# Thirteen small constants and the choice of the fixed expert, spread over pairs of heads, and four steps of the tail and the slots put elsewhere

## The chip, the core and the metric

The kernel runs on one core of a Trainium2 chip. The metric is the time of one execution on the device, in microseconds (us). Before the change it was 640.17 us, the median of three runs (639.43 to 644.14). The core's engines work from queues of their own, each in program order, and meet at semaphores: PE is TensorE (matrix products), DVE is VectorE, ACT is ScalarE, POOL is GpSimd, and SP issues most DMA transfers.

## The reference

```python
def reference(**kwargs):
    ...
    attn_out = _attn_ref(**attn_kwargs)          # 4 batches, 8 heads, 576 tokens, head size 64
    B, H, S, D = attn_out.shape
    x = attn_out.transpose(0, 2, 1, 3).reshape(B * S, H * D)      # 2304 tokens x 512
    x = _moe_ref(x=x, **moe_kwargs)
    return _moe2_ref(x=x, **moe2_kwargs)

def _attn_ref(q, k, v):                          # heads 0-3: the last 32 tokens,
    scores = scale * np.matmul(q, k.transpose(0, 1, 3, 2))        # heads 4-7: each 4th of the last 128
    scores = np.where(masks[None], scores, -1000000000.0)
    attn = np.exp(scores - scores.max(-1, keepdims=True))
    attn = attn / (np.sum(attn, axis=-1, keepdims=True) + 1e-09)
    return np.matmul(attn, v)

def _moe_ref(x, w_gate, w_output_gate, w1, w2):  # 8 experts, F = 1024, one expert for each token
    logits = x @ w_gate
    e_idx = np.argmax(logits, axis=1)
    ...
    for e in range(E):
        h = np.maximum(x[mask] @ w1[e], 0.0)
        out[mask] = gate_w[mask, None] * eom[mask, e, None] * (h @ w2[e])
```

The second MoE (`_moe2_ref`) is like the first, with a bias by modality added to the logits and without the output gate `eom`.

## The kernel before

**Attention** goes over 16 pairs of heads. `iteration(n)` is software pipelined: it holds the steps of several neighbouring pairs, in the order of a list of names written out by hand (`ORDER`). Of pair n+1 it computes scores (`stA`, 'A0' to 'A2', into `ps`), of which DVE takes row maxima `M` (line 399); POOL splits the maxima into three bf16 parts (`r`, `mb`, lines 415 to 420, step 'MS'), and PE turns them (`pm`, line 430, step 'MT') so that they can be subtracted in the transposed scores of pair n (`stB`). Of pair n-1 it computes the value product (`stC`, 'C0' and 'C1', into `po`, line 459), and DVE normalises it: `rc` (463), `recip` (465), `xh` (466). After that come the low half of `x` on POOL (481), transposes, and the router's logits (`stR`, 530 and 531). The splits of the keys (`kk`, 356) and queries (`qs`, `ql`) of pair n+2 lie between these on DVE and POOL. The order on DVE in an iteration is: two `M`, `rc`, `recip`, `xh`, `kk`, `M`, `qs`, `kk`, `ql`.

Two places in `iteration(n)` take further work: its start, ahead of the first two `M`, and the entry 'W' of `ORDER`, between `xh` and the first `kk`. At the start of iteration 3 stood `slot_consts()` and `token_values()`, 13 small operations that turn the iota tile in `cft` into tables of slot numbers (`slots`, `tokv`; 153 to 170), which only the sort needs. From iteration 8 on `fes`, the generator of `first_expert("a")`, is advanced at both places. It counts, over the first 512 tokens, which expert is chosen most: seven DVE operations on `fe_eqa` (186 to 192), a matmul `pfe` (195), four on `fe_mea` (198 to 201), five on POOL that end in the expert's number `fe_gia` (205 to 210), and three on DVE (`fe_Mia`, `fe_Msa`, `fe_owna`). At the 'DW' of iteration 10 SP reads that number and starts to load this expert's weights.

**The tail** is the last pairs' steps, written out in `tail()`, with the raw weights' splits (`los`, `his`, line 107) and `first_slots` (`fs()`, names `fs_`) among them. The latter finds 256 tokens of the fixed expert in the first 1664: it ends in a comparison `fs_A` (230), a matmul `pfs` (275), the indices `fs_fidx` (278) and two gathers on POOL.

**Each MoE** works in slots of 128 tokens of one expert. Slots 0 and 1 belong to the fixed expert; meanwhile `sort()` places all other tokens (generators `so1`, `so2`), with a matmul `pidx` (834) and `idx` (838), gathers of the first sorted slots, and the table of experts by slot that the weights are loaded by. A slot is: gathered rows turned by PE (`pxt`, 918) and copied by ACT (`xT`, 919), first product `ph` (940), ReLU and its remainder (`hh`, `hl`), second product `py` (1012), and output `y`. In the first MoE, the output is also turned (`pyt`, 1174) and sent through the second router (`plg`, 1183, added on DVE by `lg`, 1192). Weights are split into f16 halves on ACT (102) and DVE (107). `at(s, k, ...)` puts a call at place k of slot s. The first 18 slots always run (`NMIN`); the others lie in nested branches on the number of slots, each with a branch hint ahead of it. In this input the first MoE takes 23 slots and the second 19.

Of the kernel before, what the change touches and what calls it, by code (L numbers as in the profile page):

```python
# [11 lines left out]
F32 = mybir.dt.float32  # L12
# [27 lines left out]
HINT = [mybir.EngineType.PE, mybir.EngineType.DVE]  # L40
# [15 lines left out]
def fused(ctx, tc, qk, vw, wr1, w1a, w2a, mid, wr2, mbias, w1b, w2b, cf, c16, cbs, cms, cib, out, dbg=None):  # L56
# [93 lines left out]
    def slot_consts():  # L150
        v = nc.vector
        si, so = (lg2.rearrange("p s e -> p (s e)")[:, k * NSLOT:(k + 1) * NSLOT].bitcast(I32) for k in range(2))
        v.tensor_copy(si, iota_t)
        v.tensor_scalar(so, si, 1, None, op0=ALU.bitwise_and)
        v.tensor_scalar(si, si, 1, None, op0=ALU.logical_shift_right)
        v.tensor_copy(s_odd, so)
        v.tensor_copy(s_half, si)
        v.tensor_scalar(s_even, s_odd, -1.0, 1.0, op0=ALU.mult, op1=ALU.add)
        v.tensor_tensor(s_even, s_even, s_half, op=ALU.mult)
        v.tensor_scalar(s_even, s_even, -1.0, None, op0=ALU.add)  # L160
        v.tensor_scalar(s_half, s_half, KA - 1.0, None, op0=ALU.add)
        v.tensor_scalar(s_two, iota_t, 2.0, None, op0=ALU.mult)
        v.memset(s_half[:, 0:1], 0.0)
        v.memset(s_odd[:, 1:2], 0.0)
# [11 lines left out]
    def first_expert(nm, lg0, psum, fe):  # L176
# [5 lines left out]
        def T(name, shape, dt=F32):  # L182
            return const.tile(shape, dt, name=f"fe_{name}{nm}")
        sh = [P, n, E]
        mx, eq, mi, me, cnt = T("mx", [P, n]), T("eq", sh), T("mi", [P, n]), T("me", [P, E]), T("cnt", [P, E], F16)
        v.tensor_reduce(out=mx, in_=lg0, axis=AX.X, op=ALU.max)
        v.tensor_tensor(eq, lg0, mx.unsqueeze(2).to_broadcast(sh), op=ALU.is_equal)
        v.tensor_tensor(eq, eq, desc.unsqueeze(1).to_broadcast(sh), op=ALU.mult)
        v.tensor_reduce(out=mi, in_=eq, axis=AX.X, op=ALU.max)
        v.tensor_tensor(eq, eq, mi.unsqueeze(2).to_broadcast(sh), op=ALU.is_equal)  # L190
        v.tensor_reduce(out=me, in_=eq.rearrange("p t e -> p e t"), axis=AX.X, op=ALU.add)
        v.tensor_copy(cnt, me)
        yield
        pm = psum()
# [7 lines left out]
        yield  # L202
# [92 lines left out]
    with ExitStack() as actx:  # L295
# [152 lines left out]
        def stC(n, h):  # L448
# [11 lines left out]
            if h == 0:  # L460
                return
            rc = ap2.tile([QT, 2, NQ, 1], F32, name="rc")
# [100 lines left out]
        def tail():  # L563
# [25 lines left out]
            stX(a, 0)  # L589
            stX(a, 1)  # L590
            fs()
            stC(b, 1)
            fs()
            stH(b)
            fs()
# [11 lines left out]
        def iteration(n):  # L607
# [14 lines left out]
            if n == 3:  # L622
                nc.gpsimd.tensor_copy(midf, midt[:, :, 0])
                slot_consts()
                token_values()
            if n >= fe_:
                next(fes, None)
            for o in ORDER:
                if o == 'W':
                    if n >= fe_:  # L630
                        next(fes, None)
# [33 lines left out]
        actx.enter_context(tc.manual_schedule())  # L665
        for n in range(-4, NPR - 1):
            iteration(n)
# [45 lines left out]
    def sort(nm, lg, nt, inv, fe, ea, tab, scale, og, extra, gscale, start):  # L713
# [127 lines left out]
        for i in range(KA, KA + 3):  # L841
            start.gather(i)
        table()
# [48 lines left out]
    def moe(w1, w2, tab, src, parts, post, start, wpair):  # L892
# [70 lines left out]
        def slot(s, nsl=None):  # L963
# [14 lines left out]
            if NMIN - 1 <= s < NSLOT - 1:  # L978
                tc.mark_branch_hint_location(f"{start.name}{s + 1}", hint=nsl > s + 1, engines=HINT)
# [23 lines left out]
            if s >= KE:  # L1003
                post.turn(s - 1)
            hook(5)
# [5 lines left out]
            for a, w in ops:  # L1011
                nc.tensor.matmul(to, a, w, start=k == 0, stop=k == len(ops) - 1)  # L1012
                k += 1
                if k == 4:
                    hook(9)
                    if s == NMIN - 1:
                        post.router(s - 2)
# [120 lines left out]
    class Post1:  # L1138
# [38 lines left out]
        def router(self, s):  # L1177
            pl = pp.tile([P, E], F32, name="plg", tag="plg")
# [40 lines left out]
    at(0, 10, run(so1, 2))  # L1219
# [8 lines left out]
    at(2, 5, lambda: start1.first_splits(FIRST[3]))  # L1228
# [3 lines left out]
    at(2, 6, first_out(post1, start1, 1))  # L1232
# [31 lines left out]
    class Post2:  # L1264
# [27 lines left out]
        def router(self, s):  # L1292
            pass
# [9 lines left out]
    at(1, 9, run(so2, 2))  # L1303
    at(1, 7, lambda: start2.turned(KA))
# [91 lines left out]
```

## Time and profile before

| | |
|---|---|
| runs | 644.14, 639.43, 640.17 us; median 640.17 |
| profiled execution: its own time | 638.38 us |
| span of its trace | 636.6 us |
| mean granted clock of TensorE | 0.971 |
| attention and tail, to the first MoE's first product | 0 to 150.56 us |
| first MoE, to the second's first product | 150.56 to 419.86 us |
| second MoE | from 419.86 us |

One execution is profiled, and the times in the trace are counted from the span's start. The span is 1.8 us shorter than that execution's own time, and the median of the runs is 1.8 us longer than that again. A granted clock of 1.00 is the full clock of TensorE.

### The profile page before, as it was taken

The page shows a single profiled execution, that of the slowest core. Times are in us where ns is not written, and L with a number is a line of the kernel's source. Part 1 is how long each engine was busy: PE and PEld are TensorE (multiplying, and loading weights), DVE is VectorE, ACT ScalarE, POOL GpSimd, SP SyncE. Part 2 cuts the span into 40 slices and gives each one's busy share as a digit, 9 for nine tenths or more (in the row PEclk, how much of TensorE's full clock was granted, in tenths as well). Part 3 has the DMA queues.
Part 4 walks back from the last instruction along what each step waited for, and adds up shares of the span by engine and source line. Part 5 has one row for each costly group of instructions (what it writes and reads, how often), then busy time and mean ns, then how long its engine had stood idle before and what let it go on. Part 6 is the DMA issues. An engine that isn't in the chain of part 4 may idle for free. (4 is left out here: it accounts for less than half of the span.)

```text
span 636.6 us, 19375 instructions
## 1 busy us (share of the span) xinstructions
PE 589.1 (93%) x7380; PEld 456.1 (72%) x7380; DVE 359.9 (57%) x657; ACT 272.8 (43%) x370; POOL 196.1 (31%) x307
## 2 busy tenths in 40 slices
PE   3888889977999999999999999989999999999994
PEld 2868778867668677687776777856777777777772
DVE  6798898888889327944859732247530101013560
ACT  5677767773294126823538411110632111114550
POOL 2567767613151310111110610002654221212120
PEclk9799989975999999999999999999999999999998
DMA  8766668972499856996968683301994423233921
GB/s 290 243 191 194 211 198 273 293 167 72 146 357 368 226 117 180 378 243 151 266 198 221 169 153 65 69 21 36 324 323 121 99 60 93 63 91 114 300 56 37
DMA packets 100864, 114.15 MB, mean 179 GB/s; under 512 B 64399, under 2 KB 69263, under 8 KB 100752
## 3 DMA queue, kind: packets, MB, share of 16 engines
q1 hardware_dynamic: 95072, 94.89, 52.5%
q0 software_dynamic: 5280, 17.13, 9.1%
q8 instruction: 59, 0.97, 0.6%
q10 hardware_dynamic: 400, 0.72, 0.3%
q14 instruction: 53, 0.43, 0.2%
HBM read 209.13 MB, written 18.22 MB: 357 GB/s over the span
## 5 line engine op out<-in xcount | busy, mean ns | idle before, releaser
L940 PEld LDWEIGHTS <-wb 128*128 128x128 f16 x4032 | 229.7, 98 | 7.3 <-issue 1.5
L940 PE MATMUL ph<-xT,wb 128*128 128x128 f16 x3648 | 210.5, 219 | 1.1 <-ACT xT L919 1.1
L951 DVE SCALAR_TENSOR_TENSOR hl<-ph,hh 128x512 f16<-128x512 f32 x84 | 57.7, 689 | 162.8 <-ACTq L959 152.8
L1012 PE MATMUL py<-wb,hh 128*128 128x512 f16 x608 | 137.8, 379 | 0.0
L950 ACT ACTIVATE hh<-ph 128x512 f16<-128x512 f32 x84 | 50.2, 597 | 147.7 <-PE ph L940 147.3
L1012 PEld LDWEIGHTS <-hh 128*128 128x128 f16 x672 | 63.6, 98 | 68.0 <-ACT hh L950 0.3
L107 DVE SCALAR_TENSOR_TENSOR wb<-raw,wb 128x1024 f16<-128x1024 f32 (+1 forms) x80 | 104.7, 1346 | 12.7 <-ACT wb L102 11.3
L102 ACT ACTIVATE wb<-raw 128x1024 f16<-128x1024 f32 (+1 forms) x80 | 87.2, 1135 | 8.2 <-issue 2.8
L1012 PE MATMUL py<-wb,hl 128*128 128x512 f16 x304 | 72.0, 379 | 0.4 <-issue 0.4
L1012 PEld LDWEIGHTS <-hl 128*128 128x128 f16 x336 | 32.9, 98 | 40.2 <-issue 0.7
L1286 POOL DMA_INDIRECT out<-y,idx x16 | 16.2, 1010 | 98.9 <-ACTq L959 80.8
L459 PE MATMUL po<-v,pT 128*96 128x65 f32 x384 | 40.7, 258 | 0.1
L459 PEld LDWEIGHTS po<-v,pT 128*96 128x96 f32 x384 | 37.6, 174 | 0.2 <-DVE xh L466 0.2
L398 PE MATMUL ps<-kk,qs 128*96 128x128 f16 x192 | 30.0, 229 | 4.5 <-DVE qs L382 2.2
L398 PE MATMUL ps<-kk,ql 128*96 128x128 f16 x192 | 30.1, 230 | 4.2 <-DVE ql L376 4.2
L1285 ACT ACTIVATE y<-py,gsb 128x512 f32<-128x512 f32 x16 | 11.0, 687 | 52.3 <-PE py L1012 52.3
L399 DVE TENSOR_REDUCE M<-ps 96x4 f32<-96x512 f32 x48 | 31.6, 681 | 2.6 <-PE ps L398 2.0
L903 POOL DMA_INDIRECT xg<-x_dram,idxaa x23 | 24.4, 1061 | 27.6 <-DMA xT<-xg 18.0
L398 PEld LDWEIGHTS <-ql 128*96 128x96 f16 x192 | 23.5, 130 | 12.5 <-DVE ql L376 5.9
L446 ACT ACTIVATE pT<-pst 128x384 f32<-128x384 f32 x48 | 23.5, 489 | 20.4 <-PE pst L445 19.7
L443 PE MATMUL pst<-mt,msel 128*128 128x96 bf16 x192 | 29.9, 216 | 2.4 <-ACT mt L432 2.4
L398 PEld LDWEIGHTS <-qs 128*96 128x96 f16 x192 | 23.9, 130 | 8.8 <-issue 3.2
(407 smaller groups left out, 726.2 us busy)
## 6 DMA issues: line engine op xcount, KB each, us to landing
raw<-in_w1a SPq DMA_DIRECT2D x95, 512.0 KB
raw<-in_w2a SPq DMA_DIRECT2D x92, 512.0 KB
raw<-in_w1b SPq DMA_DIRECT2D x75, 512.0 KB
raw<-in_w2b SPq DMA_DIRECT2D x72, 512.0 KB
qk<-in_qk SPq DMA_DIRECT2D x16, 608.0 KB
v<-in_vw SPq DMA_DIRECT2D x16, 390.0 KB
y_dram<-y SPq DMA_DIRECT2D x11, 260.0 KB
y_dram<-lotmp SPq DMA_DIRECT2D x10, 260.0 KB
```

The source lines that it names most:

```text
L102: nc.scalar.activation(wb[:, 0, s], raw[:, s], AF.Copy, scale=SW)
L107: nc.vector.scalar_tensor_tensor(out=wb[:, 1, s], in0=raw[:, s], scalar=SW, in1=wb[:, 0, s], op0=ALU.mult, op1=ALU.subtract)
L398: nc.tensor.matmul(ps[:, j, :], q[:, h, QT * i:QT * i + QT], kk[:, h, QT * i:QT * i + 128], start=False, stop=w == 1 and j == 3, skip_grou ...
L399: nc.vector.tensor_reduce(out=Ms[n][:, 4 * g:4 * g + 4], in_=ps, axis=AX.X, op=ALU.max)
L443: nc.tensor.matmul(ps[:, j, :], msel[:, typ, j, :], mt[:, g, :], start=j == 0, stop=False, skip_group_check=True)
L446: nc.scalar.activation(pTs[n][:, 4 * g:4 * g + 4, :], ps, AF.Exp, scale=0.125 / (SQK * SQK))
L459: nc.tensor.matmul(po[:, h, i, :], pT[:, NQ * h + i, :], v[:, h, i, :], start=True, stop=True)
L903: nc.gpsimd.indirect_dma_start(t, None, src, bass.IndirectOffsetOnAxis(start.idx[:, s:s + 1], 0))
L940: nc.tensor.matmul(ph[:, j, :], w[:, c, fs], xT[:, parts[c + i], :], start=k == 0, stop=k == 47, skip_group_check=True)
L950: nc.scalar.activation(hs, ph, AF.Relu)
L951: nc.vector.scalar_tensor_tensor(out=hl[:, 4 * g:4 * g + 4, :], in0=ph, scalar=0.0, in1=hs, op0=ALU.max, op1=ALU.subtract)
L1012: nc.tensor.matmul(to, a, w, start=k == 0, stop=k == len(ops) - 1)
```

## The change

- The slot tables are made in four pieces: at the start of iteration 0, and at the 'W' of iterations 0, 1 and 2. `token_values()` is at the 'W' of iteration 3.
- The choice of the fixed expert is in smaller pieces. One product goes to POOL. Iteration 8 has two DVE operations at its start and two at 'W', iteration 9 two at its start, iteration 10 `pfe` at its start, and at 'W' the four on `fe_mea` and POOL's five; iteration 11 has the last three at its start.
- In the tail the last value product, `stC(b, 1)`, stands ahead of `stX(a, 1)`; its normalisation is a function of its own and stands behind `fs_fidx` and the gathers.
- `sort()` yields ahead of `table()`. In the second MoE its index matmul and gathers are called at place 4 of slot 1 (9 before), the table at 9; the first gathered rows are turned at place 10 (7 before).
- In slot 2 of the first MoE the weight split `FIRST[3]` stands behind the outputs of slots 0 and 1.
- In slot 17 the second router for slot 15 stands ahead of the second product, and its sums lie in the PSUM tile `pw`.
- The branch hints stand on PE alone (on PE and DVE before).

```diff
@@ constants, slot_consts()
-HINT = [mybir.EngineType.PE, mybir.EngineType.DVE]
...
         v.tensor_copy(si, iota_t)
         v.tensor_scalar(so, si, 1, None, op0=ALU.bitwise_and)
         v.tensor_scalar(si, si, 1, None, op0=ALU.logical_shift_right)
+        yield
         v.tensor_copy(s_odd, so)
         v.tensor_copy(s_half, si)
         v.tensor_scalar(s_even, s_odd, -1.0, 1.0, op0=ALU.mult, op1=ALU.add)
+        yield
         v.tensor_tensor(s_even, s_even, s_half, op=ALU.mult)
         v.tensor_scalar(s_even, s_even, -1.0, None, op0=ALU.add)
         v.tensor_scalar(s_half, s_half, KA - 1.0, None, op0=ALU.add)
+        yield
         v.tensor_scalar(s_two, iota_t, 2.0, None, op0=ALU.mult)
         v.memset(s_half[:, 0:1], 0.0)
         v.memset(s_odd[:, 1:2], 0.0)
@@ first_expert()
+        t = gp if nm == "a" else v
         v.tensor_reduce(out=mx, in_=lg0, axis=AX.X, op=ALU.max)
         v.tensor_tensor(eq, lg0, mx.unsqueeze(2).to_broadcast(sh), op=ALU.is_equal)
-        v.tensor_tensor(eq, eq, desc.unsqueeze(1).to_broadcast(sh), op=ALU.mult)
+        t.tensor_tensor(eq, eq, desc.unsqueeze(1).to_broadcast(sh), op=ALU.mult)
+        if nm == "a":
+            yield
         v.tensor_reduce(out=mi, in_=eq, axis=AX.X, op=ALU.max)
         v.tensor_tensor(eq, eq, mi.unsqueeze(2).to_broadcast(sh), op=ALU.is_equal)
+        if nm == "a":
+            yield
         v.tensor_reduce(out=me, in_=eq.rearrange("p t e -> p e t"), axis=AX.X, op=ALU.add)
         v.tensor_copy(cnt, me)
         yield
+        if nm == "a":
+            yield
         pm = psum()
         nc.tensor.matmul(pm, ones, cnt, start=True, stop=True)
         yield
...
         v.tensor_reduce(out=m, in_=me, axis=AX.X, op=ALU.max)
-        yield
+        if nm != "a":
+            yield
 
         g, gi = T("g", [P, 1]), T("gi", [P, 1], I32)
@@ stC()
-            if h == 0:
+            if h == 0 or n == NPR - 1:
                 return
+            normalise(n)
+
+        def normalise(n):
...
             rc = ap2.tile([QT, 2, NQ, 1], F32, name="rc")
@@ tail()
             stX(a, 0)
+            fs()
+            stC(b, 1)
             stX(a, 1)
             fs()
-            stC(b, 1)
             fs()
+            normalise(b)
             stH(b)
-            fs()
             stR(a - 2)
@@ iteration()
             if n == 3:
                 nc.gpsimd.tensor_copy(midf, midt[:, :, 0])
-                slot_consts()
-                token_values()
+            if n == 0:
+                next(scs)
             if n >= fe_:
                 next(fes, None)
             for o in ORDER:
                 if o == 'W':
+                    if 0 <= n < 3:
+                        next(scs, None)
+                    if n == 3:
+                        token_values()
                     if n >= fe_:
                         next(fes, None)
...
+        scs = slot_consts()
         for n in range(-4, NPR - 1):
@@ sort()
             start.gather(i)
+        yield
         table()
@@ the slots' loop
-                tc.mark_branch_hint_location(f"{start.name}{s + 1}", hint=nsl > s + 1, engines=HINT)
+                tc.mark_branch_hint_location(f"{start.name}{s + 1}", hint=nsl > s + 1, engines=PE)
...
             if s >= KE:
                 post.turn(s - 1)
+            if s == NMIN - 1:
+                post.router(s - 2, "pw")
...
                 if k == 4:
                     hook(9)
-                    if s == NMIN - 1:
-                        post.router(s - 2)
@@ router(), plan of both MoEs
-        def router(self, s):
-            pl = pp.tile([P, E], F32, name="plg", tag="plg")
+        def router(self, s, tag="plg"):
+            pl = pp.tile([P, E], F32, name=tag, tag=tag)
...
-    at(0, 10, run(so1, 2))
+    at(0, 10, run(so1, 3))
...
-    at(2, 5, lambda: start1.first_splits(FIRST[3]))
...
-    at(2, 6, first_out(post1, start1, 1))
+    at(2, 6, first_out(post1, start1, 1), lambda: start1.first_splits(FIRST[3]))
...
-    at(1, 9, run(so2, 2))
-    at(1, 7, lambda: start2.turned(KA))
+    at(1, 4, run(so2, 2))
+    at(1, 9, run(so2))
+    at(1, 10, lambda: start2.turned(KA))
```

The lines of the changed kernel are shifted by up to 25. **DVE in iteration 8**, from the choice of the fixed expert on (`fe_` names), before:

```order
L186 TENSOR_REDUCE fe_mxa<-lg_88 128x4
L187 TENSOR_TENSOR fe_eqa<-lg_88,fe_mxa 128x32
L188 TENSOR_TENSOR fe_eqa<-fe_eqa,cft 128x32
L189 TENSOR_REDUCE fe_mia<-fe_eqa 128x4
L190 TENSOR_TENSOR fe_eqa<-fe_eqa,fe_mia 128x32
L191 TENSOR_REDUCE fe_mea<-fe_eqa 128x8
L192 CAST fe_cnta<-fe_mea 128x8
L399 TENSOR_REDUCE M<-ps 96x4 x2
L463 TENSOR_SCALAR rc<-po 96x12
L465 RECIPROCAL rc<-rc 96x12
L466 TENSOR_TENSOR xh<-po,rc 96x2x6x64
L356 SCALAR_TENSOR_TENSOR kk<-qk,kk 64x608
```

and now:

```order
L189 TENSOR_REDUCE fe_mxa<-lg_88 128x4
L190 TENSOR_TENSOR fe_eqa<-lg_88,fe_mxa 128x32
L409 TENSOR_REDUCE M<-ps 96x4 x2
L479 TENSOR_SCALAR rc<-po 96x12
L481 RECIPROCAL rc<-rc 96x12
L482 TENSOR_TENSOR xh<-po,rc 96x2x6x64
L194 TENSOR_REDUCE fe_mia<-fe_eqa 128x4
L195 TENSOR_TENSOR fe_eqa<-fe_eqa,fe_mia 128x32
L366 SCALAR_TENSOR_TENSOR kk<-qk,kk 64x608
L409 TENSOR_REDUCE M<-ps 96x4
```

Of the seven operations ahead of `M` two are left there, two stand between `xh` and `kk`, and the product with `cft` is on POOL.

**DVE in the tail**, from the last operations ahead of `fs_A` on, before:

```order
L265 TENSOR_TENSOR fs_fob<-fs_fob,tokv_79 128x26
L230 TENSOR_TENSOR fs_A<-c16t,fs_fp_2504 128x1664
L463 TENSOR_SCALAR rc<-po 96x12
L465 RECIPROCAL rc<-rc 96x12
L466 TENSOR_TENSOR xh<-po,rc 96x2x6x64
L278 TENSOR_SCALAR fs_fidx<-pfs 128x2
L531 TENSOR_TENSOR lg_88<-pl,lg_88 128x80 x2
```

and now:

```order
L275 TENSOR_TENSOR fs_fob<-fs_fob,tokv_79 128x26
L240 TENSOR_TENSOR fs_A<-c16t,fs_fp_2496 128x1664
L288 TENSOR_SCALAR fs_fidx<-pfs 128x2
L479 TENSOR_SCALAR rc<-po 96x12
L481 RECIPROCAL rc<-rc 96x12
L482 TENSOR_TENSOR xh<-po,rc 96x2x6x64
L547 TENSOR_TENSOR lg_88<-pl,lg_88 128x80 x2
```

The indices `fs_fidx` have gone ahead of the normalisation (`rc` to `xh`).

**PE in slot 17 of the first MoE** (`pyt` turns an output, `py` is the second product, `plg` and `pw` the second router), before:

```order
L1174 LDWEIGHTS lotmp
L1174 MATMUL pyt<-identh,lotmp 128x128
L1012 LDWEIGHTS hh
L1012 MATMUL py<-wb_2656,hh 128x512
...
L959 UNCONDITIONAL_BRANCH
L1183 LDWEIGHTS yT_2692
L1183 MATMUL plg<-wr2h,yT_2692 128x8
```

and now:

```order
L1197 LDWEIGHTS lotmp
L1197 MATMUL pyt<-identh,lotmp 128x128
L1206 LDWEIGHTS yT_2692
L1206 MATMUL pw<-wr2h,yT_2692 128x8
...
L1037 LDWEIGHTS hh
L1037 MATMUL py<-wb_2656,hh 128x512
```

The router's products have gone ahead of the first four `py`, and into another PSUM tile.

## Rows read from the trace of the kernel before

**Rows 1.** The page's first part, TensorE: busy us (share of the span) and instructions.

```profile
PE 589.1 (93%) x7380; PEld 456.1 (72%) x7380; DVE 359.9 (57%) x657; ACT 272.8 (43%) x370; POOL 196.1 (31%) x307
```

**Rows 2.** The waits of TensorE: total us, times, longest.

```profile
PE pm L430 <- POOL mb L420: 5.1, 10, 0.6
...
PE pfe L195 <- DVE fe_cnta L192: 2.1, 1, 2.1
...
PE ph L940 <- ACT xT L919: 1.1, 1, 1.1
...
PE plg L1183 <- DVE lg L1192: 0.9, 1, 0.9
...
PE pyt L1174 <- DVE y L1156: 0.7, 1, 0.7
```

**Rows 3.** Timeline of DVE, iterations 1 to 3: start, us, instruction, [idle before <-releaser].

```profile
24.57 1.35 DVE L399 TENSOR_REDUCE M<-ps 96x4 f32<-96x512 f32 x2 [1.49 <-PE ps L398]
26.40 0.17 DVE L463 TENSOR_SCALAR rc<-po 96x12 f32<-96x12 f32 x1 [0.48 <-PE po L459]
...
33.39 0.17 DVE L463 TENSOR_SCALAR rc<-po 96x12 f32<-96x12 f32 x1 [0.98 <-PE po L459]
...
39.40 1.67 DVE L160 TENSOR_SCALAR slots<-slots 128x27 f32<-128x27 f32 x1
...
42.58 0.16 DVE L463 TENSOR_SCALAR rc<-po 96x12 f32<-96x12 f32 x1
```

**Rows 4.** Timeline of POOL, iterations 8 and 9.

```profile
77.02 1.64 POOL L481 TENSOR_TENSOR x<-xh,x 96x768 f16<-96x768 f32 x1
...
90.31 0.68 POOL L205 TENSOR_SCALAR fe_ga<-fe_ma 128x1 f32<-128x1 f32 x1
...
92.29 0.25 POOL L415 TENSOR_SCALAR r<-M 96x12 f32<-96x12 f32 x1
```

**Rows 5.** Timeline of DVE, iterations 8 to 10.

```profile
71.16 0.17 DVE L463 TENSOR_SCALAR rc<-po 96x12 f32<-96x12 f32 x1 [1.10 <-PE po L459]
...
77.07 1.63 DVE L188 TENSOR_TENSOR fe_eqa<-fe_eqa,cft 128x32 f32<-128x32 f32 x1
78.73 0.19 DVE L189 TENSOR_REDUCE fe_mia<-fe_eqa 128x4 f32<-128x32 f32 x1
...
81.49 0.16 DVE L463 TENSOR_SCALAR rc<-po 96x12 f32<-96x12 f32 x1
...
88.70 0.17 DVE L463 TENSOR_SCALAR rc<-po 96x12 f32<-96x12 f32 x1 [0.42 <-PE po L459]
...
96.41 0.17 DVE L463 TENSOR_SCALAR rc<-po 96x12 f32<-96x12 f32 x1 [0.56 <-PE po L459]
```

**Rows 6.** Timeline of DVE in the tail.

```profile
142.65 0.17 DVE L463 TENSOR_SCALAR rc<-po 96x12 f32<-96x12 f32 x1 [1.34 <-PE po L459]
```

**Rows 7.** Timeline of TensorE in the tail (weight loads apart).

```profile
140.02 0.64 PE L514 MATMUL px<-identh,x 96*128 96x96 f16 x6 [1.52 <-ACT xT L521]
140.46 2.15 PE L459 MATMUL po<-v,pT 128*96 128x65 f32 x12
142.40 0.53 PE L275 MATMUL pfs<-fs_fob,fs_A 128*128 128x2 f16 x13
```

**Rows 8.** Stretch 140 to 150: busy of each engine, granted clock, DMA share.

```profile
140.00:150.00 10.00, 7.12 (x111) 6.46 (x110) 7.95 (x16) 4.21 (x4) 3.68 (x4) 0.50 0.32 88
```

**Rows 9.** Timeline of DVE, slot 17 of the first MoE.

```profile
358.30 3.48 DVE L107 SCALAR_TENSOR_TENSOR wb<-raw,wb 128x1024 f16<-128x1024 f32 x3
```

**Rows 10.** Timeline of TensorE, slot 1 of the second MoE.

```profile
443.13 1.89 PE L1012 MATMUL pya<-wb,hl 128*128 128x512 f16 x8
444.85 0.61 PE L918 MATMUL pxt<-identh,xg 128*128 128x128 f16 x8
```

**Rows 11.** Timeline of DVE and ACT behind the first MoE's last slot.

```profile
422.40 0.75 DVE L1152 SCALAR_TENSOR_TENSOR y<-py,prg,y 128x512 f16<-128x512 f32 x1 [3.07 <-issue]
419.96 0.69 ACT L1151 ACTIVATE y<-py,prg 128x512 f16<-128x512 f32 x1 [6.11 <-SPq L1041]
```

More of the change, by code (lines that the diff above doesn't have):

```diff
@@ L459, in stC @@
                 nc.tensor.matmul(po[:, h, i, :], pT[:, NQ * h + i, :], v[:, h, i, :], start=True, stop=True)
-            if h == 0:
+            if h == 0 or n == NPR - 1:
                 return
+            normalise(n)
+        def normalise(n):
+            b, hp = divmod(n, 4)
+            xh = x_half[b, hp // 2]
+            po = pos[n][:, :, 0:65 * NQ].rearrange("q h (i c) -> q h i c", c=65)
             rc = ap2.tile([QT, 2, NQ, 1], F32, name="rc")
@@ L1290, in transposes, with router @@
             pass
-        def router(self, s):
+        def router(self, s, tag=None):
             pass
```

## The prediction

> **What bounds the kernel now.** I began with the page's busy shares: TensorE works 93% of the span [rows 1], so a microsecond comes only out of a hole of PE or out of a faster PE. Next the waits of TensorE, for the list of those holes [rows 2]; the reader should see that most are short, that four of them (`pfe`, the first product behind `xT`, `plg`, `pyt`) occur once, and that each of these lies at a place which the diff touches. The wait of `pm` for POOL's `mb` is another kind: ten times about 0.5.
>
> Then the timeline of DVE in the attention. From one `rc` to the next is one iteration: 33.39 - 26.40 = 6.99 [rows 3], and 88.70 - 81.49 = 7.21 without extra work that matters [rows 5]. This beat is a loop through four engines. `rc`, `recip`, `xh` and `kk` on DVE lead to the last scores on PE, these to the last `M`, that to POOL's `r` and `mb`, that to `pm` (the ten waits), and behind `pm` on PE's queue stands the value product for which the next `rc` waits (idle 0.48 to 1.10 "<-PE po") [rows 2, 3, 5]. So the two places that take extra work are not alike. The entry 'W', between `xh` and `kk`, is on the loop: what stands there delays it one for one. The start of an iteration, ahead of the two `M`, has the idle time in front of `rc` as its cover, 0.4 to 1.1 a time.
>
> Two iterations are long: the one that ends with `rc` at 42.58 (9.19) and the one with `rc` at 81.49 (10.33); that at 96.41 is 7.71 [rows 3, 5]. In both long ones DVE has no idle time before `rc`: it was the bound.
>
> **Slot tables.** Removed: 13 operations at the start of iteration 3, worth 9.19 - 6.99 = 2.20. They cost so much because one of them, line 160, took 1.67 [rows 3]. Added: four pieces and `token_values()`, elsewhere. A small DVE operation takes 0.19 and begins about 0.2 behind the last one (line 189) [rows 5]. The pieces of iteration 0 I take as free: before the `M` at 24.57, behind them, DVE has 1.49 of idle time [rows 3]; if that cover is gone, the second of them (three operations) costs 0.6. At the 'W' of iteration 1: 3 x 0.2 = 0.6. Of iteration 2: one operation and two fills, 0.25. Of iteration 3: `tokv`, 0.25. All three are on the loop, together 1.1. Gain: 2.20 - 1.10 = 1.1.
>
> **Fixed expert.** Removed: 10.33 - 7.21 = 3.12 in iteration 8, and 7.71 - 7.21 = 0.50 behind iteration 9, where POOL's five operations from 90.31 held back the `r` of the loop until 92.29 [rows 4, 5]; together 3.62. PE's wait of 2.1 at `pfe` goes with it; it is the same time seen from PE, and is not counted again. Added: at the starts of iterations 8, 9, 10 and 11 two DVE operations, two, a matmul and three: 0.4 to 0.6 each, under the idle time before `rc`, nothing (if the cover is gone, 0.5 each). At the 'W' of iteration 8 two operations, 0.45, and 0.25 more since POOL's product with `cft` pushes POOL's `x` and `ql` back, beside which they run: 0.7. At the 'W' of iteration 10 four operations, 0.7, and behind them POOL's five, which now begin that much later against the `r` of the loop: 0.4 more. Sum 1.8. Gain: 3.62 - 1.80 = 1.8. The expert's number is ready one iteration later, in the same iteration in which SP reads it. If SP waits for it there, what stands behind it on SP's queue are pieces of this expert's weights and the loads of later pairs; the weights are split only in the tail, so I cost it at nothing (if not, at the 0.7 by which the number's chain starts later).
>
> **Tail.** Before, the value product at 140.46 stood behind `px`, which waited 1.52 for `xT` [rows 7]. `rc` waited 1.34 for it, until 142.65 [rows 6], so DVE was done with `fs_A` at 142.65 - 1.34 = 141.31. Now the product runs in PE's hole ahead of 140.02 and has ended by then. Next late is the index path, which now stands first: `pfs` takes 0.53 [rows 7] and `fs_fidx` some 0.2, so `rc` begins at about 141.31 + 0.8 = 142.1. Gain 0.5, which the rest of the tail passes on, a chain of `xh`, `x`, `xT` and `pxa`. The bounds are 0 and 1.34.
>
> **Slots.** In slot 17 PE waits 0.9 (0.86 by the difference of its neighbours) for `lg` [rows 2], because both routers use one PSUM tile and `lg` stands behind three weight splits of 3.48 [rows 9]. With the first router in `pw` the second need not wait: gain 0.86; nothing else is late there. In slot 2 PE waits 0.7 for a `y` behind a weight split that now stands later [rows 2]; but DVE has no idle time around it, so the same work is late at the next need: I take 0 of 0 to 0.7. In the second MoE, PE waits 1.1 for `xT` [rows 2], since the turn of the gathered rows (`pxt` at 444.85) stands behind eight `hl` products of 1.89 [rows 10]. It now stands behind four of them, some 0.95 earlier, and the gather is earlier by more than that. Gain 0.95 (0.4 to 1.1). The table, later by 0.3 to 0.4, sets when weights are loaded; if they come late, that is the 0.4 below.
>
> **Branch hints.** What DVE's jump out of the nested branches costs is shown at one place: behind the first MoE DVE idles 3.07 before its first `y`, for nothing that the profile shows. ACT's half of the same output ran at 419.96 for 0.69, so its data was there at 420.65 at the latest [rows 11]: 422.40 - 420.65 = 1.75 are unexplained although DVE had its hint. PE's `pyt` waited for that `y`. Without the hint the jump can cost up to 3.07 more or give 1.75 back; the row shows a hint that didn't do its work, so I take 0.
>
> **The sum** against the profiled execution's own 638.38: 1.1 + 1.8 + 0.5 + 0.86 + 0 + 0.95 + 0 = 5.2, that is 633.2. That execution is 1.8 below the median of the runs, 640.17; I predict for the median: **634.9**.
>
> **Rivals.** *The pieces are held by POOL, and the kernel is slower.* Line 160 took 1.67 and line 188 1.63, just until POOL's `x` (77.02, 1.64) was done, and the reduction behind it 0.19 [rows 3 to 5]. Now five pieces stand at 'W' (iterations 1, 2, 3, 8, 10) on the loop, close to where POOL runs `x` and `ql`. If one operation of each is held by 1.67 - 0.17 = 1.5, that is 7.5 more, and the time 634.9 + 7.5 = 642.4. It decides from the point where the added work costs more than what is removed, 2.20 + 3.62 + 0.5 + 0.86 + 0.95 = 8.1, against 2.9 as summed above. Against it: most of POOL's `x` and `ql` are over when `xh` ends. Chance 0.05. The Trainium skill, "SBUF — State Buffer", section "SBUF: two separate sides", says that the port pair which VectorE and GpSimd share is locked for a whole instruction by a GpSimd operation, against a VectorE operation of a two-port mode or with two inputs from SBUF; the rows agree (1.63 beside 0.19 for a reduction).
>
> *The gains of attention are given back*: the pieces cost on the loop what they cost before. Then 2.3 is left: 640.17 - 2.3 = 637.9. For it speaks that 'W' is on the loop, against it that two operations of 1.6 were most of the old price [rows 3, 5]. Chance 0.12.
>
> *DVE pays for its jumps without the hint*: 1.75 to 3.07 more [rows 11], 636.7 to 638.0. Chance 0.15. The Trainium skill, "Runtime: NRT & Kernel Launch", section "Instruction fetch mechanics", speaks against this part of the change: a taken branch whose target isn't within the instructions at hand has to fetch them before work goes on. By that rule it would be this rival; that the hinted jump shows 1.75 of such a hole bears the rule out, but not the hint's use.
>
> *The hole closes instead*, since the hint's own instructions are gone: 634.9 - 1.75 = 633.1. Chance 0.13.
>
> *The half clock of the tail goes.* From 140 to 150 the granted clock is 0.50 (of 2.4 GHz, so 1.2), PE busy 7.12 [rows 8], after holes such as the 1.52. With the product in the hole PE may stay at the full clock. Estimate: of the 7.12 some 3 are on the chain of the tail, and at full clock they take 1.5 less: 633.4. Against it: most waits of the chain remain. Chance 0.15.
>
> **How the numbers follow.** The forecast itself has 0.40. The range goes from 631.3 (the closed hole and the clock together, 634.9 - 3.25, and 0.3 for the uncertain median) to 638.6 (the dearest jump, 638.0, with the 0.6 of the second slot piece). A measurement of this kernel can tell about 1%, 6.4 us, from no change. Faster by more than that, below 633.8, are the closed hole, the clock and a part of the forecast's spread: 0.35. Slower by more than that, above 646.6, only a dearer form of the first rival: 0.03. Within 1%: 0.62.
>
> **What would show it.** In the profile after, `rc` to `rc` should be 7.0 to 7.9 in every iteration from 1 to 11, no operation of `slots` or `fe_` over 1 us, and no `pfe` wait; `rc` in the tail begins right behind `fs_fidx`; the waits of `plg` and of the first product behind `xT` are gone. The prediction is wrong if iterations 1 to 3, 8 or 10 grow by more than 1 us (first rival), if DVE's idle time behind the first MoE isn't about 3 (the two on hints), or if a new wait of PE over 1 us appears in slots 1 to 3 of either MoE for weights or rows.

## The result

| | median | runs | ratio to before (95% interval) |
|---|---|---|---|
| before | 640.36 us | 4 (639.43 to 644.14) | |
| changed | 635.07 us | 4 (633.70 to 636.15) | 0.9909 (0.9880 to 0.9937) |
| changed, on another chip | 631.46 us | 6 (630.48 to 632.42); before 638.67, 17 runs | 0.9899 (0.9881 to 0.9917) |

The kernel is 5.3 us faster, 0.9% (7.2 us between the medians on the other chip, 1.0% by the ratio); predicted were 634.9 and a range of 631.3 to 638.6. The median of before has moved from 640.17 to 640.36 by a fourth run (640.55). The two traces must not be compared end to end: that of before is of an execution 2.0 below its median (638.38), that of the change of one 1.1 above (636.15), so that their spans differ by 2.3 only. Within a stage they can be compared, as far as the granted clock in it is the same.

The waits of TensorE in the changed kernel (lines are shifted by up to 25):

```profile
PE pm L440 <- POOL mb L430: 5.2, 9, 1.1
...
PE pyt L1197 <- DVE fe_meb L208: 0.8, 1, 0.8
...
PE pfe L204 <- DVE lg L547: 0.6, 1, 0.6
PE pfe L204 <- DVE fe_cntb L199: 0.5, 1, 0.5
...
PE py L1037 <- ACTq L982: 0.3, 1, 0.3
...
PE ph L963 <- ACT xT L942: 0.2, 1, 0.2
```

Of the waits of [rows 2] that of `plg` is gone, that of the first product behind `xT` has fallen from 1.1 to 0.2, that of `pfe` from 2.1 to 0.6. The longest wait for `mb` has grown from 0.6 to 1.1. The attention on DVE, `rc` (now line 479) by `rc`:

```profile
26.90 0.17 DVE L479 TENSOR_SCALAR rc<-po 96x12 f32<-96x12 f32 x1 [0.47 <-PE po L469]
...
70.40 0.17 DVE L479 TENSOR_SCALAR rc<-po 96x12 f32<-96x12 f32 x1 [1.11 <-PE po L469]
...
77.58 0.17 DVE L479 TENSOR_SCALAR rc<-po 96x12 f32<-96x12 f32 x1
...
85.36 0.17 DVE L479 TENSOR_SCALAR rc<-po 96x12 f32<-96x12 f32 x1 [0.76 <-PE po L469]
...
92.66 0.17 DVE L479 TENSOR_SCALAR rc<-po 96x12 f32<-96x12 f32 x1 [0.48 <-PE po L469]
...
102.18 0.17 DVE L479 TENSOR_SCALAR rc<-po 96x12 f32<-96x12 f32 x1 [2.33 <-PE po L469]
...
110.18 0.17 DVE L479 TENSOR_SCALAR rc<-po 96x12 f32<-96x12 f32 x1 [0.48 <-PE po L469]
...
124.57 0.17 DVE L479 TENSOR_SCALAR rc<-po 96x12 f32<-96x12 f32 x1 [0.44 <-PE po L469]
```

and before, behind the `rc` at 96.41 [rows 5]:

```profile
103.66 0.17 DVE L463 TENSOR_SCALAR rc<-po 96x12 f32<-96x12 f32 x1 [1.10 <-PE po L459]
...
125.21 0.17 DVE L463 TENSOR_SCALAR rc<-po 96x12 f32<-96x12 f32 x1 [0.44 <-PE po L459]
```

The beat that ends iteration 8, 10.33 before [rows 5], is 77.58 - 70.40 = 7.18. But the beat behind iteration 10 is 102.18 - 92.66 = 9.52, and the next 8.00, where before they were 7.25 and 7.16. POOL and PE show why (windows: the columns end in granted clock, DMA share and GB/s):

```profile
94.83 0.78 POOL L215 TENSOR_SCALAR fe_ga<-fe_ma 128x1 f32<-128x1 f32 x1 [0.90 <-DVE fe_ma L210]
...
97.50 0.86 POOL L425 TENSOR_SCALAR r<-M 96x12 f32<-96x12 f32 x1
```

```profile
94.66 1.20 PE L469 MATMUL po<-v,pT 128*96 128x65 f32 x12
...
99.78 0.42 PE L440 MATMUL pm<-identb,mb 96*128 96x96 bf16 x3 [1.11 <-POOL mb L430]
100.00 2.15 PE L469 MATMUL po<-v,pT 128*96 128x65 f32 x12
```

```profile
98.00:106.00 8.00, 6.59 (x83) 6.22 (x84) 5.42 (x14) 2.10 (x3) 5.27 (x12) 0.57 0.93 309
```

POOL's five operations take the time from 94.83 to 97.50, PE waits 1.11 for `mb`, and then the granted clock is 0.57 over 98 to 106: the value product takes 2.15 where it took 1.20. At `rc` of iteration 14 only 125.21 - 124.57 = 0.64 is left of all that attention had gained (1.14, if each is counted from its first `rc`, 26.40 [rows 3] and 26.90).

In the tail `rc` follows the index operation at once (141.99, `fs_fidx` 141.91). Behind the first MoE, DVE's first `y` has 1.28 of idle time in place of 3.07 [rows 11], and PE's wait at `pyt` is gone:

```profile
417.33 0.45 PE L1206 MATMUL plg<-wr2h,yT 128*128 128x8 f16 x12
418.43 1.96 PE L963 MATMUL ph<-xsA,wb 128*128 128x128 f16 x32 [0.65 <-DVEq L1064]
420.23 0.61 PE L1197 MATMUL pyt<-identh,y 128*128 128x128 f16 x8
420.67 1.06 PE L963 MATMUL ph<-xsA,wb 128*128 128x128 f16 x16
```

From the last `plg` to the second group of `ph` it is 420.67 - 417.33 = 3.34, before 423.44 - 418.69 = 4.75:

```profile
418.69 0.45 PE L1183 MATMUL plg<-wr2h,yT 128*128 128x8 f16 x12
...
423.44 1.06 PE L940 MATMUL ph<-xsA,wb 128*128 128x128 f16 x16
```

### The profile page after: what moved, and what is told of

The parts are those of the page before. It is cut to its first block, busy times and chain, and to the rows that moved or that the text cites. A ratio compares the mean times of both kernels' runs of the same rounds, so it can differ in the third digit from the quotient of the medians.

```text
span 634.3 us, 19356 instructions
## 1 busy us (share of the span) xinstructions
PE 590.2 (93%) x7380; PEld 455.9 (72%) x7380; DVE 357.0 (56%) x656; ACT 273.4 (43%) x370; POOL 196.3 (31%) x308
## 5 line engine op out<-in xcount | busy, mean ns | idle before, releaser
L926 POOL DMA_INDIRECT xg<-x_dram,idxaa x23 | 26.4, 1149 | 27.8 <-DMA xT<-xg 18.1
```

Source lines behind the costliest of these rows:

```text
L926: nc.gpsimd.indirect_dma_start(t, None, src, bass.IndirectOffsetOnAxis(start.idx[:, s:s + 1], 0))
```

## The experiments

Each is compared with the kernel before on its own chip. Five do one part of the change alone, four vary the changed kernel's choice of the expert, two its hints, and `after_again` is the changed kernel itself.

**hint_only**: the kernel before, and

```diff
-                tc.mark_branch_hint_location(..., engines=HINT)
+                tc.mark_branch_hint_location(..., engines=PE)
```

> The kernel before with the branch hints on PE alone, nothing else changed. Theory H (DVE's own hint makes the hole behind the first MoE): DVE's idle time before its first y there falls from 3.07 to about 1.3, PE's wait of 1.17 at pyt goes, and the second MoE ends 1.2 to 1.4 earlier in its own terms; time 1.2 to 1.4 below the kernel before, ratio 0.998. Rival S (the hole closed in the changed kernel since other edits shifted DVE's instructions): the 3.07 and the 1.17 stay, time within 0.3 of the kernel before. Rival P (a hint saves DVE's jump): the hole grows by 1.75 to 3.

Measured: 637.68 against 640.01, ratio 0.9963 (0.9951 to 0.9975), 2.3 less. DVE behind the first MoE:

```profile
421.62 0.75 DVE L1152 SCALAR_TENSOR_TENSOR y<-py,prg,y 128x512 f16<-128x512 f32 x1 [1.30 <-ACT y L1151]
```

3.07 has become 1.30, and the same stretch of PE (419.68 to 423.04) takes 3.36. Theory H holds: the hole came with DVE's hint. The time fell by 1 us more than this stretch shows; where, the one trace doesn't tell.

**after_hints_back**: the changed kernel with `engines` PE and DVE again.

> The changed kernel with the branch hints on PE and DVE again. Theory H: DVE idles about 3 behind the first MoE again and PE waits about 1.2 at pyt; time 1.2 to 1.4 above the changed kernel, about 636.4. Rival S: the hole stays closed, time as the changed kernel (635.1).

Measured: 635.66 against 640.01, ratio 0.9937 (0.9917 to 0.9957).

```profile
418.77 0.75 DVE L1175 SCALAR_TENSOR_TENSOR y<-py,prg,y 128x512 f16<-128x512 f32 x1 [3.23 <-issue]
```

The hole is back (3.23), and PE waits 1.33 at `pyt`: theory H again.

```profile
92.33 0.17 DVE L479 TENSOR_SCALAR rc<-po 96x12 f32<-96x12 f32 x1 [0.48 <-PE po L469]
...
100.82 0.17 DVE L479 TENSOR_SCALAR rc<-po 96x12 f32<-96x12 f32 x1 [1.29 <-PE po L469]
```

In this trace the beat behind iteration 10 is 100.82 - 92.33 = 8.49 at granted clock 1.00, and the next 7.16: that is the price of the work at 'W' of iteration 10 without the half clock.

**expert_only**: the kernel before with only the new `first_expert()`.

> The kernel before with only the choice of the fixed expert spread as in the change. From the trace after: 3.1 less in the iteration that ends at the eighth rc, and 2.3 plus 0.8 more in the tenth and eleventh beats after it, where POOL's five operations hold back r. Theory G (the gain is given back there): beats of 7.2, 7.8, 7.3, then 9.5 and 8.0, and the last rc of attention within 0.3 of the kernel before; time within 0.5 of it. Rival C (the long beat came from a half clock that fell in this one execution): the tenth beat is 8.1 to 8.5 and the last rc 1.5 to 2.5 earlier; time 1.5 to 2.5 less.

Measured: 639.28 against 640.01, ratio 0.9987 (0.9973 to 1.0001).

```profile
92.95 0.17 DVE L471 TENSOR_SCALAR rc<-po 96x12 f32<-96x12 f32 x1 [0.48 <-PE po L467]
102.42 0.17 DVE L471 TENSOR_SCALAR rc<-po 96x12 f32<-96x12 f32 x1 [2.28 <-PE po L467]
109.58 0.17 DVE L471 TENSOR_SCALAR rc<-po 96x12 f32<-96x12 f32 x1 [0.44 <-PE po L467]
```

9.47 again, with `mb` waited for 1.11 and a value product of 2.15, but the next beat is 7.16: the half clock lasted 3.4 us here and 6.8 in the trace of the change. So the long beat is no accident of the first trace; the half clock in it was there in four of five traces with this block (not in after_hints_back). Theory G, with 0.8 left of the gain.

**expert_early**: the changed kernel, `pfe` one place earlier.

```diff
         yield
-        if nm == "a":
-            yield
         pm = psum()
```

> The changed kernel, with the count's matmul pfe one place earlier (W of iteration 9), so that the four operations on it and POOL's five come at the start of iteration 10, where POOL runs them behind mb and ahead of x, off the loop. Theory G: no beat over 7.8 between the eighth rc and the end, PE's wait of 1.11 for mb and the half clock behind it gone; the last rc of attention about 2 to 3 earlier than in the changed kernel, as far as the last pair's own holes let it through; time 1 to 3 below 635.07. Rival C: same as the changed kernel within 0.5.

Measured: 634.95 against 640.01, ratio 0.9922 (0.9901 to 0.9944), no better than the change. The beat behind iteration 10 is 7.22 and no wait for `mb` over 0.5, as theory G says, but both theories missed what came ahead of it: the beat behind iteration 9 is 94.88 - 84.91 = 9.97.

```profile
88.44 0.55 PE L546 MATMUL pl<-wr1h,xT 128*128 128x16 f16 x15 [2.00 <-DVE lg L547]
```

`pfe` now holds one of the PSUM buffers that it shares with the router's `pl` from 'W' to the next start, so the second `pl` waits 2.00 until DVE has read the first, and from 88 to 92 the granted clock is 0.55 to 0.59. One wait had been exchanged for another.

**expert_split**: the changed kernel; only the number (`g`, `gi`, the first two of POOL's five) stays on POOL at 'W' of iteration 10, the other three operations come at the start of iteration 11, and DVE's three one iteration later.

```diff
         gp.tensor_copy(gi, g)
+        fe.update(gi=gi)
+        if nm == "a":
+            yield
         o, u = T("o", [P, E]), T("u", [P, E])
...
         yield
+        if nm == "a":
+            yield
         sh = [P, E, E]
```

> The changed kernel, with POOL's five operations on the fixed expert in two parts: the expert's number (two operations, 0.78 and 0.19) stays at W of iteration 10, the other three stand at the start of iteration 11, behind mb and ahead of x; the last three DVE operations are one iteration later. Theory G (POOL's five operations ahead of r cost the beat behind iteration 10 some 1.2, and up to 3.1 with the half clock that the wait for mb brings): the two operations end before the next M does, the beat falls from 9.5 (8.3 to 8.5 at the full clock) to about 7.9, PE's wait of 1.11 for mb is back at 0.5, no half clock there; time 1 to 2 below the changed kernel, ratio to the kernel before about 0.989. Rival D (the four DVE operations at W are the price, not POOL): the beat is as in the changed kernel and the time too.

Measured: 636.47 against 640.67, ratio 0.9944 (0.9924 to 0.9963). The beat fell to 100.19 - 92.30 = 7.89, the wait for `mb` is 0.50 and the clock full, as theory G says; but the one behind it is 110.86 - 100.19 = 10.67:

```profile
106.67 1.70 DVE L231 TENSOR_TENSOR fe_Mia<-fe_oa 128x64 f32<-128x64 f32 x1
108.30 1.31 DVE L232 TENSOR_TENSOR fe_Msa<-fe_oa 128x64 f32<-128x64 f32 x1
```

```profile
106.65 1.64 POOL L502 TENSOR_TENSOR x<-xh,x 96x768 f16<-96x768 f32 x1
108.25 1.27 POOL L393 TENSOR_TENSOR ql<-qk,qs 64x576 f16<-64x576 f32 x1
```

Two operations that took 0.21 each in the changed kernel began just behind POOL's `x` and `ql` and ended with them. It is the mechanism of my first rival, at a place where the change itself doesn't meet it. Rival D falls: the four DVE operations stand at 'W' here too.

**expert_dve**: the changed kernel; POOL keeps the number, the three operations on `fe_oa` and `fe_ua` go to DVE, at the start of iteration 11 ahead of `fe_Mia`.

> The changed kernel with only the expert's number left on POOL at W of iteration 10; the three small operations behind it run on DVE at the start of iteration 11, ahead of the three that use them, when POOL is still at mb and not at x. Theory G (POOL's block ahead of r and the meeting of DVE's two-input operations with POOL's x are the two prices): the beat behind iteration 10 is 7.9, none of the six operations takes over 0.4, the next beat is 7.2 to 7.6, and 0.5 to 1 is gained on the changed kernel (1.5 to 2.5 where that has its half clock). Rival W (any six operations there are too many for the cover): the next beat is 8.0 or more and nothing is gained.

Measured: 631.78 against 638.67, ratio 0.9916 (0.9896 to 0.9936), as the changed kernel. The beat is 101.56 - 92.34 = 9.22 at the full clock, the next 7.14:

```profile
98.66 0.23 DVE L232 TENSOR_TENSOR fe_Msa<-fe_oa 128x64 f32<-128x64 f32 x1
98.82 1.63 DVE L233 TENSOR_SCALAR fe_owna<-cft,fe_ma 128x8 f32<-128x8 f32 x1
100.36 1.27 DVE L414 TENSOR_REDUCE M<-ps 96x4 f32<-96x512 f32 x2
```

POOL's `x` had begun at 98.77. Five of six operations were cheap, the last was held for 1.63. Neither theory is whole: the half clock is gone, but the cover was 0.05 too short.

**expert_own**: expert_dve with `fe_own` moved to 'W' of iteration 10.

```diff
         v.tensor_reduce(out=m, in_=me, axis=AX.X, op=ALU.max)
+        own = T("own", [P, E])
+        if nm == "a":
+            v.tensor_scalar(own, desc, m, None, op0=ALU.is_equal)
```

> The kernel expert_dve with its sixth operation, fe_own, moved from the start of iteration 11 to W of iteration 10 (it needs only fe_ma). In expert_dve this operation began at 98.82, just behind POOL's x at 98.77, and took 1.63. Theory G (a small DVE operation with SBUF input that meets POOL's x or ql is held until that is done; the others cost 0.2 each): the five left at the start take 0.25 or less each, the beat behind iteration 10 falls from 9.2 to 8.0 to 8.2, the next is 7.2, no half clock between 95 and 110; time about 1 below expert_dve and 1 to 3 below the changed kernel, ratio to the kernel before 0.988. Rival W (whatever stands last is held, since POOL's x begins as soon as mb is done): the fifth operation takes 1.6 instead and nothing is gained.

Measured: 631.46 against 639.29, ratio 0.9876 (0.9853 to 0.9899).

```profile
99.32 0.23 DVE L235 TENSOR_TENSOR fe_Msa<-fe_oa 128x64 f32<-128x64 f32 x1
...
100.91 0.17 DVE L488 TENSOR_SCALAR rc<-po 96x12 f32<-96x12 f32 x1 [0.15 <-PE po L478]
```

```profile
83.00:87.00 4.00, 3.94 (x36) 3.72 (x37) 2.14 (x6) 2.10 (x3) 2.87 (x3) 0.57 0.55 209
```

No operation is held, the beat is 100.91 - 92.74 = 8.17 and the next 7.16, as theory G has it. But in this trace the half clock came elsewhere: from 83 to 87 the granted clock is 0.57, and the beat behind iteration 8 is 85.43 - 76.66 = 8.77 in place of 7.78. PE had no wait over 0.63 ahead of it, from 70 on. From the first `rc` to that of iteration 14 it is 96.42; the changed kernel takes 97.67 and 97.80 with its half clock, after_hints_back without it 95.76, and expert_dve 96.49. So the trace shows a gain over the changed kernel only where that has its half clock, and none over expert_dve. The ratio is the lowest of all, but its interval overlaps theirs: the time doesn't show the gain either.

**slots_only, tail_only, moe_only**: the kernel before with one other part each.

```diff
 # slots_only
-                slot_consts()
-                token_values()
+            if n == 0:
+                next(scs)
...
+                    if 0 <= n < 3:
+                        next(scs, None)
+                    if n == 3:
+                        token_values()
 # tail_only
             stX(a, 0)
+            fs()
+            stC(b, 1)
             stX(a, 1)
...
+            normalise(b)
 # moe_only
+            if s == NMIN - 1:
+                post.router(s - 2, "pw")
...
+    at(1, 4, run(so2, 2))
+    at(1, 9, run(so2))
+    at(1, 10, lambda: start2.turned(KA))
```

> The kernel before with only the slot tables spread. By the trace after: the first beats 0.5 and 0.4 longer, the beat of iteration 3 2.0 to 2.2 shorter without its 1.67 operation, tokv 0.2; 0.7 to 1.1 earlier from iteration 4 on, which the loop hands on unchanged to the last pair; ratio 0.9985. Rival L (the last pair's wait for ACT's weight splits swallows what attention gains): the beats are shorter but the last rc is not earlier, ratio 1.000.

Measured: 639.81 against 640.67, ratio 0.9987 (0.9974 to 0.9999). `rc` at 26.79, 34.17, 41.49 and 48.66; each small operation took at most 0.19 but for one cast of 0.68 at 'W' of iteration 0, `tokv` 0.25. From the first to the fourth it is 21.87, before 49.57 - 26.40 = 23.17: a gain of 1.30. From the first to the last it is 142.42 - 26.79 = 115.63, before 142.65 - 26.40 = 116.25: 0.62 is left, since the beat that ends iteration 13, at a place that the edit doesn't touch, is 7.92 here and 7.22 before. Rival L is not the reason: the last pair's beats are as before.

> The kernel before with only the last value product moved up in the tail. By the prediction: rc of the last pair begins right behind the index operation, 0.5 to 0.6 earlier, and the first product of the first MoE as much; ratio 0.999. Rival K (the clock): PE stays at the full clock through the tail and 1.5 or more is gained, ratio 0.9975. Rival N: the first product waits for another engine and comes at the same time.

Measured: 639.95 against 640.67, ratio 0.9993 (0.9980 to 1.0006).

```profile
143.79 0.16 DVE L278 TENSOR_SCALAR fs_fidx<-pfs 128x2 int32<-128x2 f32 x1 [0.60 <-PE pfs L275]
143.87 0.15 DVE L469 TENSOR_SCALAR rc<-po 96x12 f32<-96x12 f32 x1
```

`fs_A` began 142.17 here and 140.29 before, `rc` 143.87 and 142.65 [rows 6]: behind the same operation it is 1.70 in place of 2.36, 0.66 earlier. To the first product of the first MoE it is 9.98 from `fs_A`, before 10.27, and 10.44 to 10.46 in four more traces without the edit; so 0.3 to 0.5 arrives there. The half clock of the tail remains, so rival K falls. That `fs_A` is later in absolute time is no work of the edit: in this trace ACT waited 2.71 for a load, PE 2.09 for ACT (at 111.89), and the granted clock fell to 0.50 from 111 to 115, for a beat of 9.45 in place of 7.22. The time alone doesn't show a gain.

> The kernel before with only the three moves in the slots (slot 2's weight split, slot 17's router, the second MoE's sorting in slot 1). By the prediction: the wait of 0.86 at plg is gone, and of PE's wait for xT in slot 1 of the second MoE 0.95; slot 2 gives nothing; together 1.8, ratio 0.997. Rival B (the gains are late elsewhere): slot 17 gives 0.86 and is lost at the change between the MoEs, where DVE's hole is, so that at most 1 is left, ratio 0.9985 or more.

Measured: 638.79 against 640.67, ratio 0.9969 (0.9953 to 0.9985), 1.9 less.

```profile
355.27 0.61 PE L1175 MATMUL pyt<-identh,lotmp 128*128 128x128 f16 x8
355.72 0.45 PE L1184 MATMUL pw<-wr2h,yT 128*128 128x8 f16 x12
...
361.20 0.45 PE L1184 MATMUL plg<-wr2h,yT 128*128 128x8 f16 x12
361.50 1.67 PE L941 MATMUL ph<-xT,wb 128*128 128x128 f16 x27
```

```profile
355.19 0.61 PE L1174 MATMUL pyt<-identh,lotmp 128*128 128x128 f16 x8
...
362.55 5.53 PE L940 MATMUL ph<-xT,wb 128*128 128x128 f16 x96
```

From `pyt` to the next `ph` in slot 17 it is 361.50 - 355.27 = 6.23, before (the second fence) 362.55 - 355.19 = 7.36. The gain is not lost at the change between the MoEs: rival B falls.

**after_again**: the changed kernel unchanged.

> The changed kernel once more, for its time beside the kernel before on one chip and a second trace of its attention. The parts run alone add up to about 6 (2.0 for the slots, 2.4 for the hints, 0.8 each for slot tables and fixed expert, 0.4 for the tail). Theory A (the parts add): ratio 0.991. Rival C (the half clock of the first trace after is part of the change): the beat behind iteration 10 is 9.5 again at granted clock 0.50; otherwise 8.2 to 8.5 at 1.00.

Measured: 0.9899, as in the table above. The ratios of the five parts alone multiply to 0.9987 x 0.9987 x 0.9993 x 0.9969 x 0.9963 = 0.9899: within their intervals (together some 0.003 to either side) they add, theory A. The wait of 1.10 for `mb`, the half clock (0.50 from 98 to 104) and a beat of 100.59 - 91.07 = 9.52 are there again, so rival C holds too: the half clock comes with the change, though not in every execution (after_hints_back).

**no_hints**: the changed kernel without `mark_branch_hint_location`.

> The changed kernel without any branch hint, on PE neither. Theory H (a hint that holds for a branch not taken the hinted way, or comes too early, costs more than the jump): PE's wait ahead of the second MoE's first product (0.65 to 0.72) falls to 0.3 or less, time 0.3 to 1 below the changed kernel. Rival P (PE's hint saves a fetch at each slot from 18 on): PE has a new hole ahead of slots 18 to 22 or behind the last slot, 1 or more in all, time 1 to 5 above it.

Measured: 637.60 against 638.67, ratio 0.9990 (0.9975 to 1.0006); on the same chip the changed kernel took 631.46, so PE's hint is worth 6.1.

```profile
415.53 0.45 PE L1206 MATMUL plg<-wr2h,yT 128*128 128x8 f16 x12
418.48 0.44 PE L963 MATMUL ph<-xsA,wb 128*128 128x128 f16 x5 [2.51 <-PEq L1064]
420.88 3.04 PE L963 MATMUL ph<-xsA,wb 128*128 128x128 f16 x27 [1.97 <-issue]
423.72 1.06 PE L1197 MATMUL pyt<-identh,y 128*128 128x128 f16 x8
424.57 0.74 PE L963 MATMUL ph<-xsA,wb 128*128 128x128 f16 x5
```

The stretch that takes 3.34 with PE's hint takes 424.57 - 415.53 = 9.04: rival P, and 5.7 of the 6.1 lie behind the last slot; slots 18 to 22 show no new wait. Of the 5.7, 2.51 + 1.97 - 0.65 = 3.8 are the two holes; the rest goes with the granted clock, which is 0.50 from 420 to 426 behind them.

## Why the prediction was right, and where it was not

The sum of 5.2 hit the size (5.3) and 634.9 the time (633.2 and 1.8 make 635.0; the difference doesn't matter). By its own terms (the third column is 1 minus the ratio of the part alone, times the kernel before on that chip):

| term | predicted | from the traces | alone |
|---|---|---|---|
| slot tables | 1.1 | 1.3 | 0.8 |
| fixed expert | 1.8 | 1.8 at the full clock, -0.1 with the half clock | 0.8 |
| tail | 0.5 | 0.6 | 0.4 |
| slots | 1.8 | 1.1 in slot 17, 0.9 less wait in slot 1 | 2.0 |
| hints | 0 | 1.4 | 2.4 |

**Slot tables.** Right, step by step: pieces at 'W' cost what they take (beats of 7.39, 7.32 and 7.17 in the changed kernel, 0.40, 0.33 and 0.18 above 6.99; 1.1 was taken), and the 1.67 operation is gone. The pieces of iteration 0 may cost a few tenths: kernels with them have the first `rc` at 25.35 to 26.90, those without at 25.41 to 26.65, which doesn't settle it.

**Fixed expert.** What was removed came out as summed: 10.33 to 7.18 and 7.71 to 92.66 - 85.36 = 7.30, 3.56 against 3.62. The two operations at 'W' of iteration 8 cost 85.36 - 77.58 - 7.21 = 0.57 against 0.7. The step that failed is "0.7, and behind them POOL's five, 0.4 more" at iteration 10. At the full clock it is 8.49 - 7.25 = 1.24, near enough (0.64 of it is there in expert_split, where POOL's last three are gone from this place); but I had not followed the wait that it makes. PE's wait for `mb` grows to 1.11, the granted clock falls to 0.50 behind it (1.2 GHz), and the two beats cost 9.52 + 8.00 - 7.25 - 7.16 = 3.11; in expert_only, where the half clock was shorter, 9.47 + 7.16 - 7.25 - 7.16 = 2.22. I looked for the clock only in the tail, though iteration 8 before shows the same: the hole of 2.1 at `pfe` and a granted clock of 0.93 over 75 to 100. There it cost nothing: slots_only has the same hole of 2.13 and the same beat of 10.33 at a granted clock of 1.00.

**Tail.** Right in its step: `fs_A` begins at 140.29 in both traces, `pfs` and `fs_fidx` are what is late next, and `rc` begins within 0.1 of the estimate (141.99 for 142.1). But the first product of the first MoE is only 150.56 - 150.24 = 0.32 earlier in this trace, all of attention included. One more piece went to the clock: the beat that ends iteration 15 is 8.75 in place of 8.20. PE waits 1.86 for ACT's `mt` there (1.87 before); before, the half clock came 1.4 us behind that wait and lasted 3.4, now it came within it and lasted 6.8. The tail's edit alone doesn't decide that: of nine traces with it six have 8.74 or 8.75, three 8.21 to 8.32; the five without have 8.20 to 8.22.

**Slots.** Right in slot 17. In slot 2 the wait of 0.7 went, and 0.55 at `pfe` and 0.47 more at the next `pyt` came: zero, as taken. In the second MoE the wait fell by 0.86, and 0.31 of it is back at 461.22, where `py` waits for ACT (`<- ACTq L982`).

**Hints.** Here I took zero between two rivals; "the hole closes instead" (0.13) came true, with 1.4 of the 1.75. The row that bore on it was read rightly as a hole that the hint did not prevent, but I weighed the absence of the hint as the greater danger. The Trainium skill, "Runtime: NRT & Kernel Launch", section "Instruction fetch mechanics", says that a taken branch to instructions that are not at hand has to wait for a fetch. PE agrees: 9.04 without its hint, 3.34 with it. That its two holes are such fetches no run shows. DVE doesn't agree: 1.3 of idle time without the hint, until ACT's half was there, 3.1 to 3.2 with it (2.65 in no_hints, where ACT itself had waited for PE). The measurement decides, and for DVE the hint was the cost; why it was is open.

**The rival that pieces at 'W' are held by POOL** (0.05) did not come: no operation of `slots`, `tokv` or `fe_` in the changed kernel takes more than 0.67 on DVE (a cast at 'W' of iteration 0; the others at most 0.43). The mechanism is real all the same, as expert_split and expert_dve show. The Trainium skill, "SBUF — State Buffer", section "SBUF: two separate sides", says of it that GpSimd's operation has the ports which the two engines share for its whole length, and that a VectorE operation in a two-port mode, or with two inputs from SBUF, waits until it is over; the runs agree with 1.70, 1.31 and 1.63 for operations of 0.21 to 0.23, each ending within 0.1 of POOL's operation, while `TENSOR_REDUCE` on PSUM ran freely. Whether `fe_own`, with one tensor as input, ran in a two-port mode no run shows.

**The total** was thus right partly by cancellation, which is luck: the hints gave 1.4 to 2.4 that I had not counted, and the half clock took some 1.9 at iteration 10 and 0.55 at iteration 15 that I had not counted either. Two of the three signs that I had named for being wrong came: a beat behind iteration 10 longer by more than 1 us (by the clock and POOL's block, not by the first rival), and an idle time of DVE behind the first MoE of 1.28 and not about 3. The third, a new wait over 1 us in slots 1 to 3, did not. The rival that attention's gains are given back (0.12) came in part: 1.14 of 2.9 is left in the trace. The half clock of the tail (0.15) did not go. At the full clock the terms of attention and tail are right as a sum: from the first `rc` to the first MoE's first product before takes 150.56 - 26.40 = 124.16, the changed kernel 123.34 and 123.09, and after_hints_back, without the half clock at iteration 10 and with the shorter one at iteration 15, 147.39 - 26.60 = 120.79. That is 3.37 less, where 1.1 + 1.8 + 0.5 = 3.4 was forecast. Open is what decides whether the half clock comes (it stayed away in one of five traces of the same block), and why the parts alone differ from their stages in the trace by up to 1 us; with intervals of 0.8 to 1.0 us to either side this can't be settled.

## What to carry to other kernels

Work that is spread over a pipelined loop costs its own length at a place on the loop; what is off the loop, on another engine, must still end before the loop's next operation there, and here work of 1.2 us there cost up to 3.1, since in four of five traces the clock fell behind the hole. Before a small VectorE operation is placed, look at what GpSimd runs at that instant: 0.05 us later it can cost 1.6 instead of 0.2. Hints and prefetches are to be tried engine by engine: the same line was worth 6 us on one and cost 1.4 to 2.4 on another.

## What the runs showed of the hardware that I had not expected

- A hole of PE of about 1.1 us in an otherwise nearly full loop was followed by a granted clock of 0.50, for 3.4 us in one execution (expert_only) and for 6.8 in three; in a fifth with the same work the clock stayed at 1.00. The size of the hole doesn't decide it: a hole of 2.13 in slots_only was not followed by the half clock, and in expert_own it came at 83 behind waits of 0.63, 0.34 and 0.50, which the changed kernel has too (0.63, 0.34 and 0.51, from 81.62 to 83.98) at a granted clock of 1.00.
- A branch hint can cost the engine that has it: DVE 3.07 and 3.23 of idle time behind the jump with it, 1.28 and 1.30 without, where PE had its hint. PE without its own had two holes of 2.51 and 1.97.
- A VectorE operation of 8 elements in each of 128 partitions took 1.63 when it began 0.05 behind GpSimd's product over 96x768.
